# Distance bias of an attention added by VectorE for every head instead of by a TensorE product

## The chip, the cores and the metric

One core of a Trainium2 chip. The metric is the device time of one execution in microseconds; lower is better. TensorE multiplies matrices into PSUM banks, VectorE (DVE) and ScalarE (ACT) do elementwise work, GpSimd (POOL) works on SBUF, and SyncE (SP) issues most DMAs.

## The reference, cut to what matters

Attention over batch 2, 8 heads, 768 positions, 64 features, with a band of 96 local keys and 8 global ones, followed by two dense blocks that the change does not touch:

```python
scores = scale * np.matmul(q, k.transpose(0, 1, 3, 2))
...
dist = np.where(is_global & ~is_local, float(n_local), np.abs(rel).astype(np.float32))
slopes = 2.0 ** (-8.0 * (np.arange(H, dtype=np.float32) + 1) / H)
bias = -slopes[:, None, None] * dist[None, :, :]
scores = scores + bias[None, :, :, :]
scores = np.where(keep, scores, -1000000000.0)
scores = scores - np.max(scores, axis=-1, keepdims=True)
a = np.exp(scores)
a = a / (np.sum(a, axis=-1, keepdims=True) + 1e-09)
return np.matmul(a, v).astype(np.float32)
```

The slope of head h is 2 to the power -(h + 1), and the table of distances is the same for all heads.

## The kernel before, in words

**Tiling.** Batch and head make 16 heads, i = 0 to 15. A head's 768 queries are six tiles of 128, two to a step, so a head has three steps (tp = 0, 1, 2) and attention 48 (j = 3 i + tp). A query tile sees 96 keys ahead of it, 8 global keys and its own 128: 232 columns (RW); the first tile of a head only its own 128. A step's scores for both tiles share one PSUM bank, 464 columns: bank S (two buffers) in steps 0 and 1 and bank TH (one buffer) in step 2 of heads 0 to 9.

**Two ways to the scores.** `WHOLE` heads (0, 1, 4, 5, 8, 9) multiply float32 queries and keys as they are: the queries of an even head lie in one half of the partitions of a tile, those of an odd head in the other half of another, with zeros beside them, and the keys of the pair lie above each other in `scratch`. Here the queries are first scaled by -1/8 on ScalarE (`scale`, L341, and L1099 for head 0). The other heads are split into a high and a low part (`split`, L265): ScalarE makes the high query part (L307), VectorE the low one (L311), and VectorE subtracts the high from the whole keys (L91), for which the keys are loaded twice, by SP (L258) and by GpSimd's queue (`keys`, L260).

**The bias.** A product with 128x128 weights (the identity times the head's slope, `eye`, `slope` L349) and the table of distances as the moving operand writes the bias into the bank, and the score products accumulate on it: one product of 464 columns a step (L378 to L384). For steps 1 and 2 of heads 10 to 15 (`fused`) there is no such product; there GpSimd multiplies the table (232 columns) by the slope (`spread`, L354), and VectorE adds it while it takes the minimum (L402, one fused instruction for each tile). The scores are negated, so the minimum is what the softmax subtracts; elsewhere a `tensor_reduce` over the bank takes it (L407).

**The order.** Written out by hand in `run_fast`: iteration j emits scores(j), the softmax minimum of j-1, exps of j-2 (L416, ScalarE, from the bank, or from SBUF where fused), transposes of j-3 (L425), their evacuation of j-4 (ScalarE, L83), the product with V of j-5 and, at a head's end, the normalisation (L297 to L299, VectorE). Every engine runs its instructions in this order. Beside them go the split of the next head (L961 to L971: its ScalarE part at tp = 0, its VectorE part at tp = 1), the loads of heads further on, the transposition and split of the attention output, from head 10 on the first dense block's theta products (bank TH), and the conversion of float64 weights, `net.run` (L1002), a few elementwise steps on ScalarE (L99, L83) and VectorE (L103, L107, L111, L91) at a time. The weights' loads begin with `net.fetch` at j = 3 (L1000).

**The start.** `begin` loads the first pair's keys by four DMAs (L1074), head 0's queries by two, runs three matmuls on zeros (L1080), builds the table of distances from iotas, and computes a flag from the two runtime sizes by which the program branches into `run_fast`.

Of the kernel before, what the change touches and what calls it, by code (L numbers as in the profile page):

```python
# [12 lines left out]
F32 = mybir.dt.float32  # L13
# [8 lines left out]
P = 128  # L22
# [19 lines left out]
TWO32 = float(2.0 ** 32)  # L42
FUSED = 10
WHOLE = (0, 1, 4, 5, 8, 9)
# [181 lines left out]
class Attention:  # L226


    def __init__(self, net, xs):
        self.net, self.nc = net, net.nc  # L230
        n = net
        a0 = n.slot("a0", [P, SLOT], F32, "a0")
        a1 = n.slot("a1", [P, SLOT], F32, "a1")
        a2 = n.slot("a2", [P, SLOT], F32, "a2")
        w = STAGE
        self.st = [a0[:, 0:w], a1[:, 0:w]]
        vw = NV * VW
        self.v = [a0[:, w : w + vw], a1[:, w : w + vw], a2[:, 0:vw]]
        self.sS = [a2[:, vw + 2 * RW * i : vw + 2 * RW * (i + 1)] for i in range(3)]
        x = vw + 6 * RW  # L240
        self.pt = [a0[:, w + vw : w + vw + 512], a1[:, w + vw : w + vw + 512], a2[:, x : x + 512]]
        a3 = n.slot("a3", [P, SLOT], F32R, "qk1")
        self.qk = [n.head["qk0"], a3[:, 0 : 2 * S + NT * KW]]
        y = 2 * S + NT * KW
        self.E = [a3[:, y + P * i : y + P * i + P] for i in range(5)]
        x = w + vw + 512
        self.bias = [a[:, x : x + RW] for a in (a0, a1)]
        self.xs = xs
# [65 lines left out]
class FastAttention(Attention):  # L314
# [17 lines left out]
    def pair(self, i):  # L332

        self.query(i)
        for x in (i, i + 1):
            b, h = divmod(x, H)
            r = self.half(x)
            self.nc.sync.dma_start(self.net.head["scratch"][r, S:STAGE], self.net.io["qk"][b, r, h, S:STAGE])
        self.query(i + 1)

    def scale(self, i):  # L341
        q = self.whole[i % 2][self.half(i)]
        scaled(self.net, "A", None, q, q, None)

    def eye(self, i):
        h = i % H
        return self.E[h] if h < 3 else self.E[3 + i % 2]

    def slope(self, i):  # L349

        e = self.nc.gpsimd if i else self.nc.vector
        e.tensor_scalar(self.eye(i), self.net.head["ident"], 2.0 ** -(i % H + 1), None, op0=ALU.mult)

    def spread(self, i):  # L354

        if FUSED <= i < NH:
            T = self.net.head["table"][:, RW:].bitcast(F32)
            self.nc.gpsimd.tensor_scalar(self.bias[i % 2], T, 2.0 ** -(i % H + 1), None, op0=ALU.mult)

    def fused(self, j):  # L360
        return j % 3 > 0 and j // 3 >= FUSED

# [6 lines left out]
    def scores(self, j):  # L369

        i, tp = divmod(j, 3)
        net = self.net
        Q, K, T = self.Q(i), self.K(i), net.head["table"]
        sp = net.bank("TH", 1) if tp == 2 and i < NH // 2 + 2 else net.bank("S", 2)
        f = self.fused(j)
        if tp == 0:
            net.mm(sp[:, 0 : 2 * RW], self.eye(i), T, True, False)
        elif not f:  # L378
            net.mm(
                sp[:, 0 : 2 * RW].rearrange("p (u c) -> p u c", u=2), self.eye(i),  # L380
                T[:, RW:].unsqueeze(1).to_broadcast([P, 2, RW]), True, False,
            )
        if i in WHOLE:
            Q, K = self.whole[i % 2].unsqueeze(1), net.head["scratch"][:, S:STAGE]  # L384
        A = Q.shape[1]
        for u in range(2):
            t = 2 * tp + u
            if t == 0:
                o, r = sp[:, PG:RW], K[:, 0:P]
            else:  # L390
                o, r = sp[:, RW * u : RW * u + RW], K[:, KW * (t - 1) + SKIP : KW * t + P]
            for a in range(A):
                net.mm(o, Q[:, a, t * P : t * P + P], r, f and a == 0, a == 1 if f else u + a == A)
        self.state[j] = {"sp": sp}

    def softmax(self, j):
        net, s = self.net, self.state[j]
        s["nm"] = net.small.tile([P, 2], F32, tag="nm", name=net.uid("nm"), bufs=3)
        if self.fused(j):
            for u in range(2):  # L400
                c = slice(RW * u, RW * u + RW)
                self.nc.vector.tensor_tensor_reduce(  # L402
                    self.sS[j % 3][:, c], s["sp"][:, c], self.bias[j // 3 % 2], scale=1.0, scalar=3.0e38,
                    op0=ALU.add, op1=ALU.min, accum_out=s["nm"][:, u : u + 1],
                )
            return
        self.nc.vector.tensor_reduce(  # L407
            s["nm"], s["sp"][:, 0 : 2 * RW].rearrange("p (u c) -> p u c", u=2), axis=AX.X, op=ALU.min
        )

    def exps(self, j):
        s, sS = self.state[j], self.sS[j % 3]
        for u in range(2):
            c = slice(PG if j % 3 + u == 0 else RW * u, RW * u + RW)
            x = sS if self.fused(j) else s["sp"]
            self.nc.scalar.activation(sS[:, c], x[:, c], AF.Exp, bias=s["nm"][:, u : u + 1], scale=-1.0)  # L416

# [477 lines left out]
def run_fast(tc, net):  # L895
# [3 lines left out]
    mix = Mix(net, xs)  # L899
    att.slope(0)  # L900
    att.query(1)
    nc.gpsimd.memset(att.whole[1][0:D], 0.0)
    att.keys(2)
    att.load_v(0)
    att.load(2)
# [33 lines left out]
    for j in range(NJ + LAG_N + 3):  # L939
# [4 lines left out]
        if 0 <= j - LAG_SM < NJ:  # L944
            att.softmax(j - LAG_SM)
        if tp == 1 and i + 1 < NH and (i + 1 < 3 or (i + 1) % H > 2):
            att.slope(i + 1)
        if tp == 1:
            att.spread(i + 1)
        if 0 <= j - LAG_EXP < NJ:  # L950
# [114 lines left out]
def begin(nc, io, net, small, head, idle):  # L1065
# [3 lines left out]
    nc.scalar.dma_start(w, io["n"].bitcast(I32).rearrange("(o n) -> o n", o=1).to_broadcast([P, 4]))  # L1069
    first = io["qk"][0, 0:D, 0:2, S:STAGE].rearrange("d h s -> h d s")  # L1070
    keys = scratch[:, S:STAGE].rearrange("(h d) s -> h d s", h=2)
    for e, x in ((nc.sync, slice(0, 2 * KW)), (nc.sync, slice(2 * KW, NT * KW))):
        for h in range(2):
            e.dma_start(keys[h, :, x], first[h, :, x])  # L1074
    qc = (slice(0, 2 * P), slice(2 * P, S))
# [9 lines left out]
    table = small.tile([P, 2 * RW], F32R, name="table")  # L1085
    T = table[:, RW:]
    V, G, O = slice(0, NPREV), slice(NPREV, PG), slice(PG, RW)
# [9 lines left out]
    qk0 = small.tile([P, 2 * S + NT * KW], F32R, name="qk0")  # L1097
    for x in qc:
        scaled(net, "A", None, scratch[0:D, x], scratch[0:D, x], None)  # L1099

# [8 lines left out]
    fi = small.tile([1, 1], I32, name="fi")  # L1109
    f32 = table.bitcast(F32)  # L1110
    F = f32[:, RW:]
    nc.vector.tensor_scalar(flag[:, 0:1], nl[0:1], 1.0, None, op0=ALU.is_ge)
    nc.vector.scalar_tensor_tensor(flag[:, 1:2], nl[0:1], float(NPREV + 1), flag[:, 0:1], op0=ALU.is_le, op1=ALU.mult)
    nc.vector.scalar_tensor_tensor(fi, ng[0:1], float(NG), flag[:, 1:2], op0=ALU.is_le, op1=ALU.mult)
    nc.gpsimd.tensor_scalar(table[:, 0:PG], R[:, 0:PG], 0.0, BIG, op0=ALU.mult, op1=ALU.add)
    nc.vector.tensor_scalar(T, R, nl, BIG, op0=ALU.is_ge, op1=ALU.mult)
    nc.vector.tensor_tensor(T, F, R, op=ALU.max)
    nc.gpsimd.tensor_copy(table[:, O], F[:, O])
    nc.vector.tensor_scalar(T[:, G], R[:, G], ng, BIG, op0=ALU.is_ge, op1=ALU.mult)
    nc.vector.tensor_scalar(T[:, G], F[:, G], nl, None, op0=ALU.max)  # L1120
# [37 lines left out]
```

## Time and profile before

| | |
|---|---|
| median of three runs | 418.91 us (417.32 to 419.46) |
| the profiled execution | 416.43 us |
| its span, first to last instruction | 414.5 us |
| mean granted TensorE clock | 0.999 |
| instructions | 6520 |
| matmul records | 2418 |

Attention fills the span up to about 120 us, the dense blocks the rest. In the rows below PE is the matmul stream and PEld the weight loads beside it; a float32 product leaves two records. Matmuls overlap, so the mean duration of one is longer than the time it takes from its neighbours; the distance between the starts of two rows is the better measure.

### The profile page before, as it was taken

The numbers are of one execution on the slowest core, as the hardware profiler recorded it, in microseconds if no ns is written. First come the engines' busy times: TensorE is split into PE (matmuls) and PEld (weight loads), VectorE is DVE, ScalarE is ACT, GpSimd is POOL, SyncE is SP. The second block draws the span as 40 slices with busy tenths as digits, with TensorE's granted clock in tenths as the row PEclk, the third lists the DMA queues.
The fourth block names the chain that finished last, engine by engine and source line by source line (L and its number), as shares of the span: only waits on it lengthen the run. The fifth ranks groups of instructions, "written<-read, shape, count | busy, mean of one in ns | idle before, by whom it ended". The sixth has DMA issues, their size and how long they took to land.

```text
span 414.5 us, 6520 instructions
## 1 busy us (share of the span) xinstructions
PE 404.9 (98%) x2418; PEld 380.0 (92%) x2418; DVE 325.6 (79%) x611; ACT 225.2 (54%) x443; POOL 22.3 (5%) x41
## 2 busy tenths in 40 slices
PE   8899999999999999999999999999999999999994
PEld 4799999989998899999999999999999998888884
DVE  5697989898887886999989999999999999700000
ACT  4798997787786957705445236446555455200000
POOL 5011120322000000000000000000000000000000
PEclk9999999999999999999999999999999999999999
DMA  5999984875100222118366433131000000210111
GB/s 162 310 225 278 248 278 122 273 214 158 37 2 0 79 79 74 38 40 243 99 218 210 145 101 104 51 103 51 2 0 2 1 2 1 76 52 37 39 52 59
DMA packets 16297, 44.20 MB, mean 107 GB/s; under 512 B 2240, under 2 KB 2688, under 8 KB 16256
## 3 DMA queue, kind: packets, MB, share of 16 engines
q1 hardware_dynamic: 14512, 39.31, 31.9%
q0 software_dynamic: 1440, 4.18, 3.6%
q8 instruction: 21, 0.34, 0.4%
q10 hardware_dynamic: 304, 0.20, 0.2%
q14 instruction: 20, 0.16, 0.1%
HBM read 40.54 MB, written 3.15 MB: 105 GB/s over the span
## 4 chain that ended last, share of the span: by engine, by line
PE 82%; ACT 5%; DMA 5%; DVE 5%; issue 1%; SPq 0%; DVEq 0%; ACTq 0%
PE O L94 22%; PE S L94 20%; PE PT L94 14%; PE TH L94 13%; PE X L94 7%; PE PT L425 4%; DMA a<-qk 2%; DMA wst<-w_tok 1%; DMA qk<-qk 1%; PE X L549 1%; ACT z L83 1%; ACT scratch L604 1%; DVE z L91 1%; ACT scratch L602 1%; DMA words<-n 1%
## 5 line engine op out<-in xcount | busy, mean ns | idle before, releaser
L99 ACT ACTIVATE wbit<-wst 128x512 f32<-128x512 f32 (+1 forms) x38 | 23.2, 613 | 17.5 <-DMA wst<-w_tok 7.3
L94 PE MATMUL O<-a,a 128*128 128x65 f32 x236 | 29.9, 268 | 0.0
L94 PEld LDWEIGHTS O<-a,a 128*128 128x128 f32 x236 | 29.0, 192 | 0.2
L83 ACT ACTIVATE a<-PT 128x512 f32<-128x512 f32 (+1 forms) x48 | 27.2, 566 | 3.3 <-PE PT L425 2.9
L425 PE MATMUL PT<-ident,a 128*128 128x128 f32 x176 | 27.0, 272 | 0.0
L94 PE MATMUL O<-wt,z 128*128 128x384 f32 x144 | 26.9, 334 | 0.0
L94 PE MATMUL TH<-wth,xTs 128*128 128x512 f32 x96 | 26.2, 407 | 0.3 <-ACT scratch L593 0.3
L94 PE MATMUL PT<-wt,z 128*128 128x384 f32 x132 | 25.8, 335 | 0.0
L94 PEld LDWEIGHTS O<-wt,z 128*128 128x128 f32 x144 | 25.2, 188 | 0.1
L111 DVE SCALAR_TENSOR_TENSOR wbit<-wst,wbit 128x512 int32<-128x512 int32 (+1 forms) x38 | 23.9, 628 | 1.1
L107 DVE SCALAR_TENSOR_TENSOR wbit<-wst,wbit 128x512 int32<-128x512 int32 (+1 forms) x38 | 23.9, 628 | 0.9
L83 ACT ACTIVATE wt<-wbit 128x384 fp32r<-128x384 f32 x24 | 12.6, 526 | 20.7 <-DVE wbit L111 12.3
L94 PEld LDWEIGHTS PT<-wt,z 128*128 128x128 f32 x132 | 23.2, 188 | 0.0
L94 PE MATMUL S<-wt,z 128*128 128x384 f32 x120 | 22.3, 336 | 0.1
L407 DVE TENSOR_REDUCE nm<-S 128x2 f32<-128x464 f32 x26 | 16.6, 638 | 6.9 <-PE S L94 5.0
L103 DVE TENSOR_SCALAR wbit<-wbit 128x512 int32<-128x512 int32 (+1 forms) x48 | 18.9, 393 | 3.7 <-ACT wbit L99 3.6
L425 PEld LDWEIGHTS PT<-ident,a 128*128 128x128 f32 x176 | 20.5, 141 | 0.9
L94 PEld LDWEIGHTS S<-wt,z 128*128 128x128 f32 x120 | 20.9, 188 | 0.4 <-ACT scratch L593 0.4
L416 ACT ACTIVATE a<-S,nm 128x232 f32<-128x232 f32 (+1 forms) x52 | 19.5, 434 | 1.7 <-DVE nm L407 0.9
L94 PEld LDWEIGHTS TH<-wth,xTs 128*128 128x128 f32 x96 | 17.0, 189 | 3.6 <-ACT scratch L593 0.5
L94 PE MATMUL O<-x,win 128*128 128x384 f32 x96 | 17.4, 336 | 0.0
L94 PE MATMUL O<-wout,g 128*128 128x512 f32 x72 | 17.1, 390 | 0.0
(224 smaller groups left out, 990.8 us busy)
## 6 DMA issues: line engine op xcount, KB each, us to landing
wst<-w_tok SPq DMA_DIRECT2D x18, 384.0 KB, 3.6
a<-v SPq DMA_DIRECT2D x16, 357.5 KB, 4.9
wst<-w_out SPq DMA_DIRECT2D x8, 512.0 KB, 3.6
qk<-qk POOLq DMA_DIRECT2D x10, 408.0 KB, 6.9
a<-qk SPq DMA_DIRECT2D x10, 384.0 KB, 6.6
out<-scratch SPq DMA_DIRECT2D x11, 256.0 KB, 2.0
wst<-w_in SPq DMA_DIRECT2D x5, 512.0 KB, 3.5
scratch<-w_tok SPq DMA_DIRECT2D x6, 384.0 KB, 3.2
```

Source lines behind the costliest of these rows:

```text
L83: self.nc.scalar.activation(out, in_, AF.Copy)
L91: e.tensor_tensor(out, in_, hi.bitcast(F32), op=ALU.subtract)
L94: self.nc.tensor.matmul(out, l, r, start=start, stop=stop)
L99: self.nc.scalar.activation(t.bitcast(F32), w[:, 1 : w.shape[1] : 2].bitcast(F32), AF.Copy, scale=REBIAS)
L103: self.nc.vector.tensor_scalar(t, t, 3, None, op0=ALU.logical_shift_left)
L107: self.nc.vector.scalar_tensor_tensor(t, w[:, 0 : w.shape[1] : 2], 29, t, op0=ALU.logical_shift_right, op1=ALU.bitwise_or)
L111: self.nc.vector.scalar_tensor_tensor(t, w[:, 1 : w.shape[1] : 2], -(1 << 31), t, op0=ALU.bitwise_and, op1=ALU.bitwise_or)
L407: self.nc.vector.tensor_reduce(s["nm"], s["sp"][:, 0 : 2 * RW].rearrange("p (u c) -> p u c", u=2), axis=AX.X, op=ALU.min)
L416: self.nc.scalar.activation(sS[:, c], x[:, c], AF.Exp, bias=s["nm"][:, u : u + 1], scale=-1.0)
L425: self.nc.tensor.transpose(pt[:, c], sS[:, self.columns(u, a)], net.head["ident"])
L549: self.nc.tensor.transpose(xb[:, P * jj : P * jj + P], self.xs[b][:, t, P * c : P * c + P], n.head["ident"])
L602: nc.scalar.activation(a, r, AF.Abs)
```

## The change

All heads take the way that steps 1 and 2 of heads 10 to 15 took: no bias product, the bias added by VectorE in the fused add-and-minimum. The tables are made one head ahead on GpSimd, 232 columns plus 128 for a head's first tile. Unsplit heads no longer scale their queries: the fused instruction scales the sum by -1/8 and their table is divided by it. A pair's keys lie in memory as one array and come in one load. The zeros beside the first odd head's queries are written by ScalarE, the three instructions of the flag move to GpSimd, the split of head 2 moves one step later, the weights' loads begin at j = 7 and their conversion at j = 10, with added steps of it at heads 9, 10 and 16. The diff, cut to its core:

```diff
-        self.E = [a3[:, y + P * i : y + P * i + P] for i in range(5)]
...
+        self.bias = [a3[:, y + (RW + P) * i : y + (RW + P) * (i + 1)] for i in range(2)]
...
     def pair(self, i):
         self.query(i)
-        for x in (i, i + 1):
...
+        self.nc.sync.dma_start(self.net.head["scratch"][:, S:STAGE], self.net.io["pairs"][i // 2])
         self.query(i + 1)
...
-    def scale(self, i):
...
-    def spread(self, i):
...
+    def tables(self, i):
         e = self.nc.gpsimd if i else self.nc.vector
+        x = 2.0 ** -(i % H + 1) / (QSCALE if i in WHOLE else 1.0)
+        e.tensor_scalar(self.bias[i % 2], self.net.head["table"], x, None, op0=ALU.mult)
...
         sp = net.bank("TH", 1) if tp == 2 and i < NH // 2 + 2 else net.bank("S", 2)
-        f = self.fused(j)
-        if tp == 0:
-            net.mm(sp[:, 0 : 2 * RW], self.eye(i), T, True, False)
-        elif not f:
...
-                net.mm(o, Q[:, a, t * P : t * P + P], r, f and a == 0, a == 1 if f else u + a == A)
+                net.mm(o, Q[:, a, t * P : t * P + P], r, a == 0, a == A - 1)
...
     def softmax(self, j):
...
-        self.nc.vector.tensor_reduce(
-            s["nm"], s["sp"][:, 0 : 2 * RW].rearrange("p (u c) -> p u c", u=2), axis=AX.X, op=ALU.min
-        )
+        i, tp = divmod(j, 3)
+        bias = self.bias[i % 2].bitcast(F32)
+        for u in range(2):
+            c, t = slice(RW * u, RW * u + RW), bias[:, 0:RW]
+            if tp + u == 0:
+                c, t = slice(PG, RW), bias[:, RW:]
+            self.nc.vector.tensor_tensor_reduce(
+                self.sS[tp][:, c], s["sp"][:, c], t, scale=QSCALE if i in WHOLE else 1.0, scalar=3.0e38,
+                op0=ALU.add, op1=ALU.min, accum_out=s["nm"][:, u : u + 1],
+            )
...
-            x = sS if self.fused(j) else s["sp"]
-            self.nc.scalar.activation(sS[:, c], x[:, c], AF.Exp, bias=s["nm"][:, u : u + 1], scale=-1.0)
+            self.nc.scalar.activation(sS[:, c], sS[:, c], AF.Exp, bias=s["nm"][:, u : u + 1], scale=-1.0)
...
-    att.slope(0)
+    att.tables(0)
     att.query(1)
-    nc.gpsimd.memset(att.whole[1][0:D], 0.0)
+    for x in (slice(0, 512), slice(512, S)):
+        nc.scalar.activation(att.whole[1][0:D, x], net.head["zeros"][0:D, 0 : x.stop - x.start], AF.Copy)
     att.keys(2)
+    att.tables(1)
...
-        if tp == 1 and i + 1 < NH and (i + 1 < 3 or (i + 1) % H > 2):
-            att.slope(i + 1)
-        if tp == 1:
-            att.spread(i + 1)
+        if tp == 1 and 1 < i + 1 < NH:
+            att.tables(i + 1)
...
-        elif i > 0 and i + 1 not in WHOLE:
-            if tp == 0:
+        if i > 0 and i + 1 not in WHOLE:
+            x = 0 if i > 1 else 1
+            if tp == x:
                 att.split(i + 1, "  A")
-            else:
+            elif tp == x + 1:
                 att.split(i + 1, "   V")
                 att.split(i + 1, " V")
-        elif tp == 1 and i + 1 in WHOLE:
-            att.scale(i + 1)
...
-        if j == 3:
+        if j == 7:
             net.fetch()
-        if 6 < j < NJ:
-            net.run((3, 2, 3)[tp] if i > 10 else 2 if i in (3, 4, 7, 8) else (1, 0, 1)[tp])
+        if 9 < j <= NJ:
+            net.run((3, 2, 3)[tp] if i > 10 else 2 if i in (3, 4, 7, 8) else (1, i // 9, 1)[tp])
...
+    for x in (slice(0, 2 * KW), slice(2 * KW, NT * KW)):
+        nc.sync.dma_start(scratch[:, S:STAGE][:, x], io["pairs"][0, :, x])
...
-    for _ in range(3):
-        net.mm(idle, zeros[:, 0:P], zeros, True, True)
+    for x in (512, 512, 256):
+        net.mm(idle[:, 0:x], zeros[:, 0:P], zeros[:, 0:x], True, True)
...
-    nc.vector.tensor_scalar(flag[:, 0:1], nl[0:1], 1.0, None, op0=ALU.is_ge)
+    nc.gpsimd.tensor_scalar(flag[:, 0:1], nl[0:1], 1.0, None, op0=ALU.is_ge)
```

## Rows read from the trace of the kernel before

**Rows 1.** The page's engine line: busy us (share of the span), instructions
```profile
PE 404.9 (98%) x2418; PEld 380.0 (92%) x2418; DVE 325.6 (79%) x611; ACT 225.2 (54%) x443; POOL 22.3 (5%) x41
```

**Rows 2.** Windows: heads 2 to 9, heads 6 to 8, heads 10 to 15
```profile
core 0: us, PE busy (x) PEld busy (x) DVE busy (x) ACT busy (x) POOL busy (x), PEclk, DMA share, GB/s
17.10:67.21 50.11, 50.11 (x405) 48.76 (x404) 42.62 (x82) 43.88 (x100) 7.33 (x10) 1.00 0.90 246
41.87:60.74 18.87, 18.87 (x159) 18.46 (x158) 17.63 (x34) 17.20 (x40) 4.40 (x5) 1.00 0.95 271
67.21:116.50 49.29, 48.88 (x355) 44.78 (x354) 42.85 (x112) 37.91 (x87) 8.93 (x12) 1.00 0.54 158
```

**Rows 3.** Chain that ended last, at the start: start us, us, what
```profile
6.45 6.93 DMA a<-qk
13.40 0.84 ACT qk L307
```

**Rows 4.** Groups by form, whole span: the bias products
```profile
L94 PE MATMUL S<-table,qk 128*128 128x464 f32 x26 | 11.8, 454 | 0.6 <-DVE qk L352 0.5
...
L94 PE MATMUL TH<-table,qk 128*128 128x464 f32 x10 | 4.7, 466 | 1.9 <-ACT a L416 1.9
```

**Rows 5.** Timeline of PE: start us, us; one split step with, one without the product
```profile
24.61 0.45 PE L94 MATMUL S<-table,qk 128*128 128x464 f32 x1
24.90 0.60 PE L94 MATMUL S<-qk 128*128 128x232 f32 x4
25.34 0.60 PE L425 MATMUL PT<-ident,a 128*128 128x128 f32 x4
...
74.86 0.69 PE L94 MATMUL S<-qk 128*128 128x232 f32 x4
75.39 0.60 PE L425 MATMUL PT<-ident,a 128*128 128x128 f32 x4
```

**Rows 6.** Timeline of the start
```profile
7.44 0.45 PE L94 MATMUL S<-table,qk 128*128 128x464 f32 x1 [0.50 <-DVE qk L352]
...
14.98 0.47 PE L94 MATMUL TH<-table,qk 128*128 128x464 f32 x1 [1.90 <-ACT a L416]
...
15.26 1.01 DVE L91 TENSOR_TENSOR qk<-a,qk 64x816 fp32r<-64x816 f32 x1
...
17.10 0.46 PE L94 MATMUL S<-table,qk 128*128 128x464 f32 x1
```

**Rows 7.** Timeline of VectorE: the minimum and its successor, the fused one and its
```profile
54.13 0.64 DVE L407 TENSOR_REDUCE nm<-TH 128x2 f32<-128x464 f32 x1
54.68 0.95 DVE L91 TENSOR_TENSOR xTs<-xT,xTs 128x768 fp32r<-128x768 f32 x1
...
73.75 0.40 DVE L402 CUSTOM_DVE_ANT_0 a<-S,a 128x232 f32<-128x232 f32 x1
...
74.07 0.56 DVE L87 CAST xTs<-xT 128x768 fp32r<-128x768 f32 x1
```

**Rows 8.** Groups by form: exps from PSUM and SBUF (whole span), scalings (heads 2 to 9)
```profile
L416 ACT ACTIVATE a<-S,nm 128x232 f32<-128x232 f32 x36 | 15.4, 460 | 1.6 <-DVE nm L407 0.9 <-DVE rs L297 0.5
...
L416 ACT ACTIVATE a<-a,nm 128x232 f32<-128x232 f32 x24 | 10.4, 488 | 2.4 <-DVE nm L402 2.4
...
L307 ACT ACTIVATE scratch<-scratch 64x768 f32<-64x768 f32 x2 | 1.7, 848 | 0.6 <-DMA scratch<-qk 0.6
L307 ACT ACTIVATE xs<-xs 64x768 f32<-64x768 f32 x2 | 1.7, 842 | 0.0
```

**Rows 9.** Timelines: a spread, a subtraction beside it; its group in the whole span
```profile
74.31 0.96 POOL L358 TENSOR_SCALAR a<-table 128x232 f32<-128x232 f32 x1 [0.41 <-DVE nm L402]
...
74.54 0.73 DVE L91 TENSOR_TENSOR wt<-wbit,wt 128x384 fp32r<-128x384 f32 x1
...
L91 DVE TENSOR_TENSOR wt<-wbit,wt 128x384 fp32r<-128x384 f32 x24 | 13.4, 559 | 1.8 <-ACT wt L83 1.8
```

**Rows 10.** DMA issues (KB, median us to landing) and timeline: the first weights
```profile
wst<-w_theta SPq DMA_DIRECT2D x4, 512.0 KB, 9.3
...
9.17 1.46 SPq L133 DMA_DIRECT2D wst<-w_theta  x2
...
21.11 0.69 ACT L99 ACTIVATE wbit<-wst 128x512 f32<-128x512 f32 x1
```

More of the change, by code (lines that the diff above doesn't have):

```diff
@@ L42 @@
 TWO32 = float(2.0 ** 32)
-FUSED = 10
 WHOLE = (0, 1, 4, 5, 8, 9)
@@ L244, in __init__ @@
         y = 2 * S + NT * KW
-        self.E = [a3[:, y + P * i : y + P * i + P] for i in range(5)]
-        x = w + vw + 512
-        self.bias = [a[:, x : x + RW] for a in (a0, a1)]
+        self.bias = [a3[:, y + (RW + P) * i : y + (RW + P) * (i + 1)] for i in range(2)]
         self.xs = xs
@@ L334, in pair @@
         self.query(i)
-        for x in (i, i + 1):
-            b, h = divmod(x, H)
-            r = self.half(x)
-            self.nc.sync.dma_start(self.net.head["scratch"][r, S:STAGE], self.net.io["qk"][b, r, h, S:STAGE])
+        self.nc.sync.dma_start(self.net.head["scratch"][:, S:STAGE], self.net.io["pairs"][i // 2])
         self.query(i + 1)
-    def scale(self, i):
[L342 to L349, printed above, removed]
-        e = self.nc.gpsimd if i else self.nc.vector
-        e.tensor_scalar(self.eye(i), self.net.head["ident"], 2.0 ** -(i % H + 1), None, op0=ALU.mult)
-    def spread(self, i):
[L356 to L361, printed above, removed]
+    def tables(self, i):
+        e = self.nc.gpsimd if i else self.nc.vector
+        x = 2.0 ** -(i % H + 1) / (QSCALE if i in WHOLE else 1.0)
+        e.tensor_scalar(self.bias[i % 2], self.net.head["table"], x, None, op0=ALU.mult)
     def chunks(self, tp):
@@ L372, in scores @@
         net = self.net
-        Q, K, T = self.Q(i), self.K(i), net.head["table"]
+        Q, K = self.Q(i), self.K(i)
         sp = net.bank("TH", 1) if tp == 2 and i < NH // 2 + 2 else net.bank("S", 2)
-        f = self.fused(j)
-        if tp == 0:
-            net.mm(sp[:, 0 : 2 * RW], self.eye(i), T, True, False)
-        elif not f:
-            net.mm(
-                sp[:, 0 : 2 * RW].rearrange("p (u c) -> p u c", u=2), self.eye(i),
-                T[:, RW:].unsqueeze(1).to_broadcast([P, 2, RW]), True, False,
-            )
         if i in WHOLE:
@@ L398, in softmax @@
         s["nm"] = net.small.tile([P, 2], F32, tag="nm", name=net.uid("nm"), bufs=3)
[L399 to L406, printed above, removed]
-        self.nc.vector.tensor_reduce(
-            s["nm"], s["sp"][:, 0 : 2 * RW].rearrange("p (u c) -> p u c", u=2), axis=AX.X, op=ALU.min
-        )
+        i, tp = divmod(j, 3)
[8 more added lines that the diff above has]
+            )
     def exps(self, j):
@@ L1069, in begin @@
     nc.scalar.dma_start(w, io["n"].bitcast(I32).rearrange("(o n) -> o n", o=1).to_broadcast([P, 4]))
[L1070 to L1074, printed above, removed]
+    for x in (slice(0, 2 * KW), slice(2 * KW, NT * KW)):
+        nc.sync.dma_start(scratch[:, S:STAGE][:, x], io["pairs"][0, :, x])
     qc = (slice(0, 2 * P), slice(2 * P, S))
@@ L1079, in begin @@
     nc.vector.memset(zeros, 0.0)
-    for _ in range(3):
-        net.mm(idle, zeros[:, 0:P], zeros, True, True)
+    for x in (512, 512, 256):
+        net.mm(idle[:, 0:x], zeros[:, 0:P], zeros[:, 0:x], True, True)
     nc.vector.memset(scratch[D:P, 0:S], 0.0)
     R = scratch[:, STAGE : STAGE + RW]
-    table = small.tile([P, 2 * RW], F32R, name="table")
-    T = table[:, RW:]
+    table = small.tile([P, RW + P], F32, name="table")
+    T, X = table[:, 0:RW], table[:, RW:]
     V, G, O = slice(0, NPREV), slice(NPREV, PG), slice(PG, RW)
@@ L1097, in begin @@
     qk0 = small.tile([P, 2 * S + NT * KW], F32R, name="qk0")
-    for x in qc:
-        scaled(net, "A", None, scratch[0:D, x], scratch[0:D, x], None)
     f = small.tile([P, 8], F32, name="nf")
@@ L1109, in begin @@
     fi = small.tile([1, 1], I32, name="fi")
-    f32 = table.bitcast(F32)
-    F = f32[:, RW:]
-    nc.vector.tensor_scalar(flag[:, 0:1], nl[0:1], 1.0, None, op0=ALU.is_ge)
-    nc.vector.scalar_tensor_tensor(flag[:, 1:2], nl[0:1], float(NPREV + 1), flag[:, 0:1], op0=ALU.is_le, op1=ALU.mult)
-    nc.vector.scalar_tensor_tensor(fi, ng[0:1], float(NG), flag[:, 1:2], op0=ALU.is_le, op1=ALU.mult)
-    nc.gpsimd.tensor_scalar(table[:, 0:PG], R[:, 0:PG], 0.0, BIG, op0=ALU.mult, op1=ALU.add)
+    nc.gpsimd.tensor_scalar(flag[:, 0:1], nl[0:1], 1.0, None, op0=ALU.is_ge)
+    nc.gpsimd.tensor_scalar(flag[:, 1:2], nl[0:1], float(NPREV + 1), flag[:, 0:1], op0=ALU.is_le, op1=ALU.mult)
+    nc.gpsimd.tensor_scalar(fi, ng[0:1], float(NG), flag[:, 1:2], op0=ALU.is_le, op1=ALU.mult)
     nc.vector.tensor_scalar(T, R, nl, BIG, op0=ALU.is_ge, op1=ALU.mult)
-    nc.vector.tensor_tensor(T, F, R, op=ALU.max)
-    nc.gpsimd.tensor_copy(table[:, O], F[:, O])
+    nc.vector.tensor_tensor(T, T, R, op=ALU.max)
+    nc.gpsimd.tensor_copy(X, T[:, O])
     nc.vector.tensor_scalar(T[:, G], R[:, G], ng, BIG, op0=ALU.is_ge, op1=ALU.mult)
-    nc.vector.tensor_scalar(T[:, G], F[:, G], nl, None, op0=ALU.max)
-    nc.vector.tensor_tensor(table[:, PG : PG + NG], f32[:, PG : PG + NG], F[:, G], op=ALU.min)
+    nc.vector.tensor_scalar(T[:, G], T[:, G], nl, None, op0=ALU.max)
+    nc.vector.tensor_tensor(X[:, 0:NG], X[:, 0:NG], T[:, G], op=ALU.min)
     nnl = small.tile([P, 1], F32, name="nnl")
-    head.update(scratch=scratch, qk0=qk0, table=table, ident=ident, half_pi=hp[:, 0:1], ng=ng, nl=nl, nnl=nnl, flag=fi)
+    head.update(scratch=scratch, zeros=zeros, qk0=qk0, table=table, ident=ident, half_pi=hp[:, 0:1], ng=ng, nl=nl, nnl=nnl, flag=fi)
 def kernel(q, k, v, n_global, n_local, moe_w_theta, moe_w_tok_r, moe_w_tok_i, moe_w_ch, moe2_w_in, moe2_conv_w, moe2_w_out):
@@ L1134 @@
     qk = np.concatenate([q.transpose(0, 3, 1, 2), kT.reshape(B, D, H, NT * KW)], axis=3)
+    pairs = kT.reshape(B, D, H // 2, 2, NT * KW).transpose(0, 2, 3, 1, 4).reshape(NH // 2, P, NT * KW)
     va = np.stack([np.concatenate([v[:, :, P * t - NPREV : P * t], v[:, :, 0:NG]], axis=2) for t in range(1, NT)], axis=3)
@@ L1140 @@
     arrays = {
+        "pairs": f(pairs),
         "qk": f(np.concatenate([qk, qk], axis=1)),
```

## The prediction

> **What bounds the kernel now.** First the page's engine line: TensorE is busy 98% of the span [rows 1], so a product taken out counts unless something else comes due just behind it. Then the windows cut at the heads. In heads 2 to 9 (17.10 to 67.21) TensorE has no gap, VectorE is busy 42.62 of 50.11 us and ScalarE 43.88; in heads 6 to 8 VectorE has 17.63 of 18.87; in heads 10 to 15 it has 42.85 of 49.29 [rows 2]. So TensorE is the bound and VectorE stands close behind it, closest in heads 6 to 8. The third view is the chain at the start: it runs through the load of head 2's queries, 6.93 us from its issue at 6.45, and ScalarE's split of them, which begins as they land [rows 3].
>
> **The bias products: -6.0.** They are 26 into S and 10 into TH, 36 in all: every step of heads 0 to 9 and the first of heads 10 to 15 [rows 4]. Their busy time there (454 to 466 ns) is not their price, because matmuls are pipelined. I compare two steps of split heads that are alike but for the product. From the start of the bias product to the first transpose is 25.34 - 24.61 = 0.73 us; without it, from the first score product, 75.39 - 74.86 = 0.53 [rows 5]. The price is 0.20. Unsplit heads have no step without one; their product has the same shape, and I take the same. The six steps of heads 0 and 1 lie ahead of head 2's gate (next part), so 30 count: 30 x 0.20 = 6.0. The rest of a step's products stays.
>
> **The start: -0.8, between 0 and -2.4.** Scores will no longer wait for the table or the scaled identity, and the queries' scaling goes. But head 2 can't start before its split is done, and that hangs on the load: landed at 13.4, ScalarE until 14.24, VectorE's two instructions until 15.26 + 1.01 = 16.27. Now head 2 starts at 17.10 [rows 6], because ScalarE, standing at the split, held back head 1's exps, and TensorE stood 1.90 us at 14.98 [rows 6]. With that split one step later these exps go first, and what is late next is the split itself: 17.10 - 16.27 = 0.8 is gained. Nothing, if the loads come as much later; 2.4 (the 1.90, and the 0.50 that the first product waits for its identity) if they come earlier. I take 0.8, since the loads ahead in SP's queue stay and the program's branch, which releases them, still waits for a flag made by three tiny instructions, on GpSimd instead of VectorE. VectorE's three are freed; TensorE's shorter idle products, the loads of the first keys in two issues instead of four, and ScalarE's zeroing of the half query all end before the gate: 0, hidden by the load of head 2 and worth at most the same 2.4 if that cover went.
>
> **VectorE: +1.0.** A minimum over 464 columns holds VectorE 0.55 us (54.13 to the next instruction at 54.68). A fused add-and-minimum of 232 holds it 0.32 (73.75 to 74.07), though each shows 0.40 [rows 7]. Two are 0.64, so a step with two full ones costs +0.09. Of the 128-column one no row exists: between 0.16 and 0.32; the two lengths above give 0.23 / 232 = 1 ns a column, so 0.32 - 0.10 = 0.22, and the first step of a head then costs 0.54, -0.01. In heads 2 to 9 that is 16 x 0.09 - 0.1 = +1.3: VectorE 43.9, TensorE 50.11 - 24 x 0.20 = 45.3. On the whole it still fits. In heads 6 to 8 it doesn't: VectorE 17.63 + 6 x 0.09 = 18.2, TensorE 18.87 - 9 x 0.20 = 17.07, 1.1 too much; I take 1.0, since a step's softmax runs some steps ahead of its transposes. Bounds: 0, if the surplus spreads over neighbours, and 2.5 (first rival). The fused minimum also takes over a wait: it writes the tile that the exp wrote, so it stands until the transposes of the head before have read it, which TensorE runs right behind the scores, 0.60 us [rows 5]. Behind it on VectorE stand splits, normalisation and weight conversions, and ScalarE's exps wait for it; the steps between exps and transposes cover that once, and if they didn't it would be part of the 2.5. In heads 10 to 15 VectorE gains nothing to do and TensorE loses 1.2 of 6 us of slack: 0.
>
> **ScalarE: 0.** An exp costs 488 ns from SBUF against 460 from PSUM: over the 40 full ones of heads 2 to 9 that newly read SBUF +1.1. Four scalings of 842 to 848 ns there go: -3.4 [rows 8]. It falls to about 41.6 of 45.3. Also, the fused minimum lets go of the PSUM bank, where the exp did; the next scores no longer wait on ScalarE. Bound: a gain of the 0.8 that heads 6 to 8 lose.
>
> **GpSimd's tables: +0.5, between 0 and 1.4.** 128-column identities and six 232-column spreads become one 360-column table a head. A spread took 0.96, so a table is about 0.96 x 360 / 232 = 1.5 us, every 5 to 6 us, needed three steps later; behind it on the queue stand only the keys' loads of the head after next. While a spread ran, VectorE's subtraction took 0.73, against 0.56 on the mean [rows 9]: 0.17. Eight tables of heads 2 to 9 make 1.4, of which the three where VectorE is short count.
>
> **The later weights: +0.3, between 0 and 3.6.** The two w_theta loads are issued at 9.17 now and ScalarE first reads one at 21.11; the median landing is 9.3 us [rows 10]. After the change ScalarE reads three steps after the issue, 3 x (50.11 / 24 - 0.20) = 5.7 us, so in its queue it can stand up to 9.3 - 5.7 = 3.6, with exps and evacuations behind it. I take 0.3, near the low end: the loads of head 4 come out ahead, and TensorE has scores of two steps to go on with. The order of the conversions shifts by three steps, and the total is made up by the steps added at heads 9, 10 and 16: 0. The pair's keys in one load save an SP issue of about half a microsecond at heads 4 and 8, on a queue that waits mostly for buffers: 0.
>
> **Sum:** -6.0 - 0.8 + 1.0 + 0.5 + 0.3 = -5.0. The profiled execution took 416.43 us (span 414.5), so 411.4. The median of the three runs is 418.91, 2.48 above; the forecast on that scale is **413.9**. After attention nothing changes, and its TensorE stream follows the last head.
>
> **Rivals.** *VectorE becomes the bound throughout.* For it: 17.63 of 18.87, and dependent instructions don't touch; 98 instructions in heads 2 to 9 with 0.03 each make 43.9 into 46.8, over TensorE's 45.3: 1.5 of loss, and 2.5 with the surplus of heads 6 to 8 that nothing then evens out. Against it: most instructions start with no gap now. With the tables at their 1.4, 6.0 + 0.8 - 2.5 - 1.4 - 0.3 = 2.6 of gain is left: 413.8, or 416.3 on the median's scale. *The late weights land on the path and the start brings nothing:* 6.0 - 1.0 - 0.5 - 3.6 = 0.9 is left, 418.0. For it: ScalarE works strictly in order, and heads 2 to 4 load without a pause. *The products were hidden:* no change, 418.9; the two steps above speak against it. *GpSimd's tables hold VectorE for their whole length, slower.* For it: the slowed subtraction ended at 74.54 + 0.73 = 75.27, and the spread at 74.31 + 0.96 = 75.27 [rows 9]. Then heads 2 to 9 cost VectorE 43.9 + 8 x 1.5 = 55.9 against 50.11, +5.8, and heads 10 to 15 42.85 + 5 x 1.5 = 50.4 against 49.29, +1.1; with the start's 0.8 that is 416.43 + 6.1 = 422.5, or 425.0. It decides from (50.11 - 43.9) / 8 = 0.8 us lost per table. Against it: a hold lasts from the instruction's start to the table's end, and most instructions beside a spread kept their length.
> The Trainium skill ("SBUF — State Buffer", "Who interferes with whom") says that a VectorE instruction with two SBUF inputs and a GpSimd instruction that reads SBUF exclude each other: whichever issues second fully blocks until the first is done. By that rule this rival is the mechanism, and the trace agrees in the one pair of ends; but the fused minimum has one input in PSUM, which by the same section doesn't contend, and with the holds only where the rule has them the sum stays near +0.5 instead of +12.
>
> **The numbers.** A measurement of this kernel can tell some 0.5%, 2.1 us, from no change. Forecast 0.66; VectorE throughout 0.18 (0.14 of it faster, 0.04 within 0.5%); late weights 0.06 and hidden products 0.02, both the same; the tables' hold 0.06, slower; better than all terms 0.02. Faster 0.82, same 0.12, slower 0.06. The range goes from the start's best without losses, 418.91 - 8.4 = 410.5, to 1.0 over the first rival, since its terms are the least known: 417.3.
>
> **What would show it.** Right: no product of 464 columns; split steps of 0.53 from first score to first transpose in heads 2 to 9; head 2 at about 16.3 and head 10 some 5 us earlier than 67.21; VectorE's 48 fused pairs at 0.32 a slot, and gaps of TensorE in heads 6 to 8 of about a microsecond, released by the fused minimum. Wrong: TensorE waiting for ScalarE at the first weight conversion; a granted clock under full after the wait for head 2; VectorE instructions stretched to a table's end; or TensorE idle through heads 2 to 9 while VectorE never is.

## The result and the profile after

The changed kernel takes 423.13 us (median of four, 422.06 to 425.05) against 418.69 before (417.32 to 419.46): 1.0115 of it, 95% interval 1.0069 to 1.0161. It is slower, where 413.9 was forecast. The profiled execution took 422.06 us, its span is 420.3 against 414.5. Ratios leave out single executions more than 1.5% above the fastest of their kernel; medians have them in.

First the page of the changed kernel: the engine line, and the row of its 40 slices that tells of TensorE's clock.

```profile
PE 408.2 (97%) x2382; PEld 384.7 (92%) x2382; DVE 328.0 (78%) x716; ACT 223.5 (53%) x438; POOL 27.6 (7%) x39
...
PEclk9856999999999999999999999999999999999998
```

There are 36 matmul records fewer than in [rows 1], as there should be, and yet TensorE is busy 3.3 us longer. Slices two to four, 10 to 42 us, show why: the granted clock is 0.8, 0.5 and 0.6 there; in the profiled execution of the kernel before every slice has 0.9 or more. The trace's clock record has it at the full level, 2.4 GHz, from 11.02 to 17.85 us, at the half level, 1.2 GHz, to 38.33, and at the full one from there to 417.21.

Next, windows cut at the heads: heads 2 to 4, heads 5 to 9, and from head 10 to the scores of attention's last step (columns as in [rows 2]). First the changed kernel, then the kernel before.

```profile
17.41:43.61 26.20, 26.20 (x141) 25.85 (x142) 14.94 (x54) 14.94 (x34) 3.85 (x4) 0.61 0.70 205
43.61:72.26 28.65, 28.65 (x240) 28.04 (x239) 27.88 (x92) 24.98 (x57) 8.73 (x8) 1.00 0.72 220
72.26:121.65 49.39, 47.86 (x349) 43.91 (x348) 45.15 (x140) 39.24 (x89) 8.71 (x9) 1.00 0.62 175
```

```profile
17.10:35.40 18.30, 18.30 (x153) 17.90 (x152) 14.83 (x30) 16.32 (x37) 2.41 (x4) 1.00 1.04 283
35.40:67.21 31.81, 31.81 (x255) 30.86 (x254) 27.79 (x53) 27.56 (x64) 4.92 (x6) 1.00 0.82 225
67.21:116.47 49.26, 48.84 (x354) 44.75 (x354) 42.82 (x112) 37.88 (x87) 8.93 (x12) 1.00 0.54 159
```

So the 5.8 us of span are: head 2 starts 0.3 later; heads 2 to 4 take 26.20 instead of 18.30, +7.9; heads 5 to 9, at full clock, take 28.65 instead of 31.81, -3.2; heads 10 to 15 take the same; the rest after them, +0.6. One stretch lost more than all the others could gain.

The timeline of the changed kernel around its beginning (start us, us, engine, instruction):

```profile
14.74 0.78 PE L93 MATMUL O<-a 128*128 128x65 f32 x6
17.41 0.77 PE L93 MATMUL S<-qk 128*128 128x128 f32 x4 [1.89 <-ACT a L384]
17.98 0.84 PE L393 MATMUL PT<-ident,a 128*128 128x128 f32 x3
18.61 1.81 PE L93 MATMUL O<-a,a 128*128 128x65 f32 x8
20.18 1.18 PE L93 MATMUL S<-qk 128*128 128x232 f32 x4
21.16 1.05 PE L393 MATMUL PT<-ident,a 128*128 128x128 f32 x4
22.01 1.81 PE L93 MATMUL O<-a,a 128*128 128x65 f32 x8
23.58 1.18 PE L93 MATMUL TH<-qk 128*128 128x232 f32 x4
```

TensorE ends head 1, stands 1.89 us for head 2's split, and half a microsecond after it begins again the clock is at half. From there a split step takes 23.58 - 20.18 = 3.4 us, and its four score products 0.98 until the first transpose, where [rows 5] have 0.53.

### The profile page after: what moved, and what is told of

The parts are those of the page before. It is cut to its first block, busy times and chain, and to the rows that moved or that the text cites. A ratio compares the mean times of both kernels' runs of the same rounds, so it can differ in the third digit from the quotient of the medians.

```text
span 420.3 us, 6500 instructions
## 1 busy us (share of the span) xinstructions
PE 408.2 (97%) x2382; PEld 384.7 (92%) x2382; DVE 328.0 (78%) x716; ACT 223.5 (53%) x438; POOL 27.6 (7%) x39
## 4 chain that ended last, share of the span: by engine, by line
PE 82%; DVE 7%; ACT 5%; DMA 3%; issue 1%; SPq 0%; DVEq 0%; ACTq 0%
PE O L93 22%; PE S L93 20%; PE PT L93 14%; PE TH L93 13%; PE X L93 7%; PE PT L393 4%; DMA a<-qk 2%; DMA wst<-w_tok 1%; DVE z L90 1%; PE X L517 1%; DVE a L375 1%; ACT a L384 1%; ACT scratch L561 1%; ACT z L82 0%; DVE qk L90 0%
## 5 line engine op out<-in xcount | busy, mean ns | idle before, releaser
L384 ACT ACTIVATE a<-a,nm 128x232 f32<-128x232 f32 (+1 forms) x96 | 40.2, 470 | 10.2 <-DVE nm L375 10.1
L375 DVE CUSTOM_DVE_ANT_0 a<-S,qk 128x232 f32<-128x232 f32 (+1 forms) x76 | 25.6, 370 | 11.0 <-PE PT L393 8.7
L93 PE MATMUL O<-a,a 128*128 128x65 f32 x236 | 33.6, 289 | 0.0
L93 PEld LDWEIGHTS O<-a,a 128*128 128x128 f32 x236 | 33.1, 215 | 0.2
L393 PE MATMUL PT<-ident,a 128*128 128x128 f32 x176 | 29.9, 293 | 0.0
L393 PEld LDWEIGHTS PT<-ident,a 128*128 128x128 f32 x176 | 22.6, 152 | 1.1 <-issue 0.2
L339 POOL TENSOR_SCALAR qk<-table 128x360 fp32r<-128x360 f32 x15 | 19.1, 1274 | 62.0 <-DVE nm L375 61.9
L93 PE MATMUL S<-qk 128*128 128x232 f32 (+1 forms) x104 | 18.5, 304 | 2.7 <-ACT a L384 1.9
```

What stands on the lines that cost most here:

```text
L93: self.nc.tensor.matmul(out, l, r, start=start, stop=stop)
L339: e.tensor_scalar(self.bias[i % 2], self.net.head["table"], x, None, op0=ALU.mult)
L375: self.nc.vector.tensor_tensor_reduce(self.sS[tp][:, c], s["sp"][:, c], t, scale=QSCALE if i in WHOLE else 1.0, scalar=3.0e38, op0=ALU.add ...
L384: self.nc.scalar.activation(sS[:, c], sS[:, c], AF.Exp, bias=s["nm"][:, u : u + 1], scale=-1.0)
L393: self.nc.tensor.transpose(pt[:, c], sS[:, self.columns(u, a)], net.head["ident"])
```

## The experiments

Theory A: the clock fell because TensorE stood still ahead of head 2. Theory B: it fell, or stayed down, because the steps of split heads are too light without the bias product. Theory C: the time went to VectorE, and the clock is a side effect.

**Filling the wait.**

```diff
+FILL = 2
...
+        if j == 6:
+            z, x = net.head["zeros"], net.bank("X")
+            for _ in range(FILL):
+                net.mm(x, z[:, 0:P], z, True, True)
```

> The changed kernel with two extra float32 products of 512 columns on zeros (results unused) on TensorE just ahead of head 2's scores, where it stands 1.89 us with nothing to do. Theory A, the granted clock falls because of this standing still: the clock stays at the full level from 11 us on, heads 2 to 4 lose none of the 9.7 us that they lose now, about 413.5 us. Theory B, it falls because the steps of heads 2 and 3 are too light without the bias product: the clock still goes to half at about 18 us, about 423 to 424 us. Theory C, the time is lost to VectorE and the clock is a side effect: no change, 423 us.

412.26 us, 0.9853 of the kernel before (0.9790 to 0.9917). In the profiled execution the clock is full from 4.52 to 407.29 us, through all of attention. Windows of the same three stretches:

```profile
17.18:33.63 16.45, 16.45 (x141) 16.24 (x142) 13.48 (x54) 14.03 (x34) 3.86 (x4) 1.00 0.95 290
33.63:62.28 28.65, 28.65 (x240) 28.03 (x239) 28.12 (x92) 25.14 (x58) 8.74 (x8) 1.00 0.79 242
62.28:111.95 49.67, 47.84 (x349) 43.91 (x348) 45.15 (x140) 39.24 (x89) 8.72 (x9) 1.00 0.60 174
```

Heads 2 to 4 take 16.45 instead of 26.20: the clock alone cost 9.75 us. The other two stretches are as in the changed kernel, 28.65 and 49.67. C falls: VectorE's instructions are the same. One of its four executions took 421.3 us, at a mean clock of 0.979, so two products fill the wait only just; 1.03 us of it are left.

**The product back in heads 2 and 3 alone, the wait left.**

```diff
+        if i in (2, 3):
+            x = net.bank("X")
+            net.mm(x[:, 0 : 2 * RW], Q[:, 0, 0:P], K[:, 0 : 2 * RW], True, True)
```

> The changed kernel with one product of 464 columns a step put back in heads 2 and 3 alone (six in all, written to a bank that nobody reads, results unused), and the wait ahead of head 2 left as it is. Theory A (the wait lowers the clock): half level from about 18 us as now; as long at half level or somewhat shorter, 420 to 424 us. Theory B (light steps lower it or keep it low): full level throughout heads 2 to 4, or back at full within a few us, 423.1 - 9.7 + 6 x 0.2 = about 414.6 us. Theory C: 423 us.

414.37 us, 0.9896 (0.9830 to 0.9963). Neither theory is right by itself. In the profiled execution the clock does fall, at 16.68, inside the wait of 3.00 us; but it is back at full at 23.51, in the second step of head 2, where the changed kernel waited until head 4. Timeline of the end of the wait, and of that step and the next:

```profile
17.39 0.73 PE L93 MATMUL X<-qk 128*128 128x464 f32 x1 [3.00 <-ACT a L387]
...
20.95 0.73 PE L93 MATMUL X<-qk 128*128 128x464 f32 x1
21.48 1.03 PE L93 MATMUL S<-qk 128*128 128x232 f32 x4
22.32 1.05 PE L396 MATMUL PT<-ident,a 128*128 128x128 f32 x4
23.16 1.17 PE L93 MATMUL O<-a,a 128*128 128x65 f32 x8
24.15 0.45 PE L93 MATMUL X<-qk 128*128 128x464 f32 x1
```

So in this execution the standing still lets the clock fall, before any step of head 2 has run, and the steps with the product bring it back early. The four executions are of two kinds: two took 416.61 (the profiled one) and 416.11 us at a mean clock of 0.989, and two 412.62 and 412.34 at 0.997 and 1.000, as fast as the filled run. In these two the clock can't have been at half for more than about 2.5 us in all (0.003 of 412 us, twice); why not is not shown, since their waits were not recorded.

**The flag on VectorE again.**

```diff
-    nc.gpsimd.tensor_scalar(flag[:, 0:1], nl[0:1], 1.0, None, op0=ALU.is_ge)
...
+    nc.vector.tensor_scalar(flag[:, 0:1], nl[0:1], 1.0, None, op0=ALU.is_ge)
...
```

> The changed kernel with the flag's three instructions back on VectorE. The flag was ready at 6.24 us against 4.65 before; they took 0.22, 0.57 and 0.28 us on GpSimd against 0.15 each. Expected by all theories: SP's loads start some 1.2 us earlier, head 2 at about 16.3 instead of 17.41. By A and B the wait ahead of head 2 stays about as long, the clock still falls, and the run gains about 1 us, 422; if the wait shortens below what lowers the clock, about 412.

422.59 us, 1.0129 (1.0092 to 1.0165). SP's loads start at 6.02 instead of 6.90, 0.9 earlier. Head 2 doesn't: its queries, issued at 7.23 instead of 8.11, land at 15.15 instead of 14.41, and TensorE stands 4.54 us. The clock is at half from 17.20 to 37.68. The expectation of 16.3 was a miss: an earlier issue did not bring an earlier landing. Why is not shown. GpSimd's keys were issued 0.03 us behind this load, in the changed kernel 0.67 ahead; but the landing also scatters between runs with the same loads in the same order (next experiment).

**The kernel before with the later split.**

```diff
-        elif i > 0 and i + 1 not in WHOLE:
-            if tp == 0:
+        if i > 0 and i + 1 not in WHOLE:
+            x = 0 if i > 1 else 1
+            if tp == x:
                 att.split(i + 1, "  A")
-            else:
+            elif tp == x + 1:
```

> The kernel before with nothing changed but the split of head 2 one step later, as in the changed kernel. Head 1's products then run before the wait, and TensorE stands right ahead of head 2, until the split is done at about 16.3, for 2 to 3 us, with the bias products kept. Theory A (the wait alone lowers the clock): it falls at about 18 us and the kernel is some 5 to 10 us slower than before, 424 to 428 us. Theory B (light steps): the clock stays full and head 2 starts up to 0.8 us earlier, 418 us. Theory C: 418 us.

417.25 us, 0.9975 (0.9944 to 1.0006), full clock. No evidence for B, though: the wait that I wanted didn't come about. In this run the load, issued at 6.42, had landed by 11.38, and head 2 started at 14.94 with no gap. In the kernel before the same load, issued at 6.45 behind the same others, landed at 13.38: 2.0 us of scatter, as much as the whole wait. So the next one makes the wait in another way.

**The kernel before with a longer wait.**

```diff
     att.load_v(0)
+    att.load_v(1)
     att.load(2)
-    att.load_v(1)
```

> The kernel before with its bias products, but the load of head 2 put behind the load of the second V, so that TensorE stands before head 2 for longer than the 1.90 us it stands now, by about the 1.5 us that a V takes to land. Theory A+B (standing still lets the clock fall, and only steps without the bias product keep it down): it falls to half at about 17 us, is back at full within some 7 us, as in the changed kernel with the product put back in heads 2 and 3 (half from 16.68 to 23.51), and costs 1.5 for the wait and 2 to 4 for the clock, 421 to 424 us. Theory B alone (no fall while the products are there): full throughout, 419 to 420 us.

420.93 us, 1.0080 (1.0026 to 1.0134). TensorE stands 4.34 us, and the clock falls with the bias products in place, at 17.00, while it still stands; it is back at 20.41. Windows of the wait, the steps after it and the following ones:

```profile
14.00:17.40 3.40, 0.00 (x1) 0.01 (x1) 0.71 (x1) 1.59 (x4) 0.00 (x0) 0.94 1.13 250
17.40:21.00 3.60, 3.60 (x16) 3.24 (x16) 2.54 (x4) 2.62 (x7) 0.00 (x0) 0.58 1.03 315
21.00:30.00 9.00, 9.00 (x79) 8.89 (x78) 7.29 (x13) 7.85 (x19) 0.00 (x0) 1.00 0.92 211
```

B as the cause of the fall is out. B as what holds it down fits this execution and two others (mean clocks of 0.993, 0.994 and 0.995); but the fourth took 430.97 us at 0.968, as low as the changed kernel's. Where it lost the clock was not recorded, so it is not shown that the bias products always bring it back soon.

**The changed kernel with the split where it was.**

```diff
-            x = 0 if i > 1 else 1
+            x = 0
```

> The changed kernel with the split of head 2 where it was before the change (ScalarE's part at the first step of head 1). TensorE then stands in head 1, as before, and has the third step of head 1 (unsplit) to run after the wait. If the place of the wait is what lets the clock fall: full level throughout, about 413 to 414 us. If its length and the light steps after it are: still half for 7 to 20 us, 418 to 423 us.

423.54 us, 1.0160 (1.0116 to 1.0205): no help. The wait is in head 1 then, and the clock at half from 16.20 to 40.09. As the wait is also longer there (2.97 us), the run tells only that its place in head 1 does not save the clock.

**The start as before, with the filling products.** The flag on VectorE, the first keys in four loads (the lines of the kernel before, L1070 to L1074), and the two products.

> The changed kernel with the two filling products ahead of head 2 (412.26 us), the flag on VectorE again and the first pair's keys in four loads of 64 partitions again. In every run with the two loads of 128 partitions the two sizes land at 4.01 to 4.10 us, in both with four at 3.30; with this the flag should be ready at about 4.7 as before, SP's loads start at 5.3 instead of 6.9, and head 2 start at 16 to 16.5 instead of 17.18: 411 to 411.5 us. If the landing of head 2's load is set by what else is on the way and not by its issue (as in the run with the flag alone, issued 0.9 earlier and landed 0.7 later): 412 to 413 us.

This one undid the cure in three of four executions: 422.27, 413.82, 420.80 and 422.06 us, at mean clocks of 0.972, 0.997, 0.979 and 0.976. The loads do start at 5.32. But the queries of head 2 land at 14.05 all the same, the products of heads 0 and 1 are over earlier, and TensorE stands 2.48 us behind the filling; in the profiled execution the clock is at half from 18.26 to 38.74. An earlier start made the wait longer and the kernel slower. Both of the effects that I expected were about a microsecond; what came was about ten.

**Fewer conversion steps at heads 9 and 10, wait filled.**

```diff
-            net.run((3, 2, 3)[tp] if i > 10 else 2 if i in (3, 4, 7, 8) else (1, i // 9, 1)[tp])
+            net.run((3, 2, 3)[tp] if i > 10 else 2 if i in (3, 4, 7, 8) else (1, 0, 1)[tp])
```

> The changed kernel with the two filling products (412.26 us), without the added conversion steps at heads 9 and 10. In the filled run TensorE stands 0.87 and 0.11 us at 69.5 and 71.5, released by the fused minimum, and stretches its spacing there by 1.4 us. If VectorE's queue is the bound there and the added steps are what overfills it: 411 to 411.5 us. If the stall hangs on the keys of head 11, which land 0.34 us late for VectorE at 67.4: 412.3 us, no change.

413.61 us, 0.9917 (0.9874 to 0.9961); its span is 410.9 against 410.7 of the filled run. TensorE's waits for the fused minimum shrink and move, to 0.68 at 68.74 and 0.21 at 77.02, but nothing is gained at the end. Heads 10 to 15 take 49.25 us, against 49.39 in the changed kernel, 49.67 in the filled run and 49.29 in the run with the early load below, all three with these steps. A gain of half a microsecond could not be told from that scatter; the stall itself is still there, so the added steps alone don't make it.

**Three filling products.** The first edit with `FILL = 3`.

> The changed kernel with three filling products of 512 columns ahead of head 2 instead of two. With two, TensorE still stood 1.03 us there and one of four executions took 421.3 us, as if its clock had fallen. If the length of standing still decides: no such execution among these, median 411.5 to 412.5 us. If it does not: one in four again at 420 us or more.

412.54 us, 0.9900 (0.9868 to 0.9932); none of ten executions over 413.99, mean clocks 0.996 to 1.000; in the profiled one TensorE no longer stands ahead of head 2. As expected where the length of standing still decides.

**No filling, but head 2's load first.**

```diff
+    att.load(2)
     att.load_v(0)
-    att.load(2)
     att.load_v(1)
```

> The changed kernel, no filling products, but with the loads of head 2 issued ahead of the first V on SP's queue. Head 2's queries then land about 1.3 to 2 us earlier, at 12.5 instead of 14.4, and TensorE stands about 1 us instead of 1.9 to 3. If the wait is the cause of the fall, whatever fills or shortens it: the clock stays full and the run takes 411 to 412.5 us without any work added. If the filling products helped because they are heavy: still half for some 20 us, 421 to 423 us.

412.07 us, 0.9892 (0.9857 to 0.9926). The queries land at 11.02, TensorE stands 0.82 us, the clock is full from 10.54 to 406.48, and no product was added. Timeline of the wait and windows of the three stretches:

```profile
14.31 0.78 PE L93 MATMUL O<-a 128*128 128x65 f32 x6
15.92 0.68 PE L93 MATMUL S<-qk 128*128 128x128 f32 x4 [0.82 <-ACT a L384]
```

```profile
15.92:32.34 16.42, 16.42 (x142) 16.22 (x142) 13.93 (x54) 14.15 (x34) 3.85 (x4) 1.00 1.01 316
32.34:60.98 28.64, 28.64 (x239) 28.04 (x239) 27.87 (x92) 24.96 (x57) 8.73 (x8) 1.00 0.76 234
60.98:110.27 49.29, 47.87 (x349) 43.93 (x348) 44.97 (x140) 39.33 (x89) 8.87 (x9) 1.00 0.62 176
```

This tells the wait from the filling: what helps is that TensorE doesn't stand, not the heaviness of what is put there. Like the filled run it beats both kernels, and by an exchange of two loads alone.

**Both.**

> Both: head 2's loads first and two filling products (1.7 us). If the wait is down to about 1 us already, the products overfill it by 0.5 to 1 us and this is that much slower than the loads first alone, 412 to 413 us; if the loads do not come earlier it equals the filled run, 412.3 us.

412.09 us, 0.9894 (0.9846 to 0.9942): the filling adds nothing once the load is early, and costs nothing that can be told.

**The kernel before with head 2's load first.**

> The kernel before with the same exchange of loads: its stall of 1.90 us ahead of the last step of head 1 should shrink to about nothing. If TensorE bounds all that follows: 1 to 2 us faster than before, about 415.5 to 416.5 us where before has 417 to 418.5. No effect of the clock is expected, which is full there already.

416.42 us, 0.9991 (0.9962 to 1.0021): no difference that can be measured, where 1 to 2 us were expected, although TensorE no longer stands ahead of head 2 in the profiled execution. So the exchange is no measurable gain of its own; its worth in the changed kernel is the clock.

## Why the prediction was wrong

**What failed.** The part on the start counted TensorE's standing still at its own length, "worth at most the same 2.4 if that cover went". It cost 9.75 us more, because the clock fell with it and the steps of heads 2 and 3 did not bring it back; forecast and result are 9.2 us apart. Where the wait is filled or shortened (412.26 and 412.07 us) the clock stays and the loss is gone. A granted clock under full stood in the prediction only as a sign of being wrong, with no price and no chance among the rivals, although the same change took the widest product out of the steps that follow the wait and shortened the idle products ahead of it.

**The start itself** was -0.8 and came out at +0.3. Two steps of it failed, and the timeline of the changed kernel shows one:

```profile
4.98 0.22 POOL L1072 TENSOR_SCALAR flag<-nf 1x1 f32<-1x1 f32 x1 [2.79 <-DVE nf L1068]
...
5.30 0.57 POOL L1073 TENSOR_SCALAR flag<-nf,flag 1x1 f32<-1x1 f32 x1
...
5.96 0.28 POOL L1074 TENSOR_SCALAR fi<-nf,flag 1x1 int32<-1x1 f32 x1
...
6.90 0.55 SPq L327 DMA_DIRECT2D xs<-qk  x1
```

"Three tiny instructions, on GpSimd instead of VectorE" take 1.3 us from the first start to the last end, where VectorE took 0.5 in the kernel before (4.14 to 4.65). And the two loads of the first keys, which I set at 0, delay the two sizes that the flag is made of: they land at 3.99 to 4.10 us in every run with two loads of 128 partitions and at 3.29 to 3.34 in every run with four of 64. Together SP's loads start 1.6 us later, 6.90 against 5.30. That the late loads made the wait is not shown, since the run with the start restored waits longer still; that it depends on the order of the loads is: put ahead of the first V, head 2's queries land 3.76 to 4.08 us after their issue in three runs, behind one V 4.96 to 7.92 in ten. The 1.89 us of the changed kernel's profile are short by chance. Its clock came to the full level only at 11.02, so heads 0 and 1 ran on until 15.52; in the run with the product put back, which is the same program up to there, it was full from 6.44, they ended at 14.39, and with the queries landing at the same time (14.39 against 14.41) TensorE stood 3.00.

**The products** were right in heads 2 to 9, which take 45.10 us in the filled run against 50.11 [rows 2]: 5.01 for 24 products, 0.21 each against 0.20. A split step at full clock has the forecast 0.53 from the first score to the first transpose (56.67 and 57.20 in the changed kernel).

**VectorE's** +1.0 came at another place and only in part by VectorE. In heads 6 to 8, where I took it, nothing is lost: they take 17.01 us in the filled run, where TensorE alone was forecast at 17.07; heads 5 to 9 take 28.65, less by 0.21 for each of their 15 products, with VectorE busy 27.88. It is lost in heads 10 to 15, which I set at 0: six products less and no time less, 49.39 against 49.26, so 1.3 us, and 1.2 to 1.7 over the changed kernel, the filled run and the one with the early load. In these three TensorE stands there 0.55 to 0.87 us for the fused minimum and 0.7 to 0.9 for ScalarE, where the kernel before stands 0.3, for ScalarE. In the filled run the fused minimum waits in VectorE's queue behind the split of the next head, whose second part in turn waited for its keys:

```profile
67.42 1.00 DVE L91 TENSOR_TENSOR qk<-a,qk 64x816 fp32r<-64x816 f32 x1 [0.34 <-DMA qk<-qk]
...
68.74 0.39 DVE L380 CUSTOM_DVE_ANT_0 a<-S,qk 128x232 f32<-128x232 f32 x1
...
69.51 0.71 PE L94 MATMUL S<-qk 128*128 128x128 f32 x4 [0.87 <-DVE nm L380]
```

But the keys are not what it hangs on. In the changed kernel the same part starts without a wait for them, and TensorE stands 0.67 us all the same:

```profile
76.01 0.95 DVE L308 SCALAR_TENSOR_TENSOR qk<-a,qk 128x768 fp32r<-128x768 f32 x1
77.00 1.01 DVE L90 TENSOR_TENSOR qk<-a,qk 64x816 fp32r<-64x816 f32 x1
...
78.43 0.38 DVE L375 CUSTOM_DVE_ANT_0 a<-S,qk 128x232 f32<-128x232 f32 x1
...
79.19 0.71 PE L93 MATMUL S<-qk 128*128 128x128 f32 x4 [0.67 <-DVE nm L375]
```

Taking two conversion steps away there gained nothing either. What is left is the order of VectorE's queue, the two parts of the split ahead of the fused minimum; no run moves them, so that is only argued.

**GpSimd's tables** took 1.27 us each (page: L339, 15 of them, 1274 ns on the mean), less than the 1.5 taken. Beside one, at 71.62 for 1.27 us in the filled run, a VectorE step with two SBUF inputs, started at 71.84, took 0.84 where its group has 0.59 on the mean; it ended at 72.68, ahead of the table's end at 72.89. The rival that a table holds VectorE for its whole length is not what made the kernel slow, though its 425.0 lies near the result: heads 5 to 9 would have shown it, and they gained all that was forecast.

**ScalarE and the late weights** cost nothing that shows: ScalarE is busy 24.98 of 28.65 us in heads 5 to 9, and in the filled run it stands 0.67 us for the first weights, with no gap of TensorE behind it.

Without the fall, the sum was close: -5.0 forecast, against a ratio of 0.9892 for the version with the early load, 4.5 us. In part that is luck: the 1.5 that VectorE and the tables were to cost in heads 2 to 9 did not come, and about as much was lost in heads 10 to 15, where nothing was forecast.

## What to carry to other kernels

When a change takes work out of a busy TensorE, price not only the work but what its absence leaves: look for the places where the engine stands, and for what the steps behind them still run. Here a wait of two to three microseconds cost ten. Once the clock row of the page shows a dip, find the wait ahead of it, and shorten it, or fill it, before looking at anything else. Moving the load was the better cure here: the filling of fixed length failed again as soon as an earlier start made the wait longer.

## What the hardware showed unexpectedly

A TensorE that the profile counts as busy without a gap can stay at the half level. In the changed kernel it was busy 9.58 of 9.58 us from 26.54 to 36.12 at a granted clock of 0.50:

```profile
26.54:36.12 9.58, 9.58 (x47) 9.58 (x47) 4.57 (x17) 4.45 (x11) 0.78 (x1) 0.50 0.30 93
```

These are split heads without the bias product: short products, most of them of 65 or 128 columns. The full level came back with the unsplit head 4, whose float32 scores are longer; with a 464-column product in each step it came back within two steps of head 2, in the profiled execution. The same split steps in heads 6 and 7, entered at the full level, kept it.

The Trainium skill ("TensorE: Matmul & The Clock Gate", "HAM oscillation — how this bites in real kernels") says that waits for DMAs between short stretches of matmuls throttle the gate, so that the next stretch starts cold. The trace agrees: half level right behind the wait for head 2. Its section "What's actually happening" says that activity releases the throttle; here an engine that the profile shows busy without a gap, from 17.41 us on, was not released until 38.33, and the measurement decides.

Standing still is not the whole rule either. The profiled execution of the kernel before stood 1.90 us [rows 6] and kept its clock; that of the changed kernel stood 1.89 and lost it, 0.44 us after TensorE had begun again. What else it takes stays open: what ran ahead of the wait differed (the full level had come at 7.20 and at 11.02), and so did what ran behind it. Over all runs the profiled executions that lost the clock at this wait had stood 1.89 to 4.54 us, those that kept it 1.90 or less; in four of the six that lost it, it fell while TensorE still stood.

Nor did the kernel before always keep it. In the batches that the experiments are compared with, 34 of its 47 executions had a mean clock of 0.997 or more and a median of 416.54 us; 11 had 0.992 to 0.994 and a median of 418.95. So its median of 418.91, which the forecast was scaled by, 2.48 above the profiled execution, lies where executions with a short loss of the clock lie. Where these lost it was not recorded.
